# A chunk of a linear-attention kernel loaded as two transfers of whole rows from two queues

## The chip, the cores and the metric

The kernel runs on one core of one Trainium2 chip. The metric is the device time of one execution in microseconds (us); the kernel before takes 338.18 us, the median of three runs (337.67 to 339.53).

## The reference

Two layers follow each other. The first is a linear attention with a decaying state (the form known from RWKV), for 4 batches, 8 heads, 768 positions and a head size of 48; the second is a mixture of 8 experts over the 3072 rows that come out of it, where each row with a positive skip score goes to the one expert that its logits choose.

```python
for t in range(S):                                    # attention, S = 768
    cur = einsum('bhd,bhe->bhde', u[None] * kt, vt)   # kt, vt, rt, wt: (b, h, d) at t
    y[:, :, t] = einsum('bhd,bhde->bhe', rt, state + cur)
    state = wt[:, :, :, None] * state + einsum('bhd,bhe->bhde', kt, vt)
...
e_idx = argmax(xc @ w_gate, axis=1)                   # experts, rows with x @ w_skip > 0
h = maximum(xc[mask] @ w1[e], 0.0)
y[mask] = gate_w[mask, None] * (h @ w2[e])
out[do_compute] = xc + y
```

## The kernel before

**The work and its tiles.** The attention is done in 24 chunks, one for each batch and each block of 128 positions, in the order of `seq` (L61). A chunk's inputs w, r, k and v lie with the head dimension on the partitions: the eight heads are four pairs side by side in the columns, the even head of a pair on partitions 0 to 47, the odd one on 64 to 111 (partitions 48 to 63 and 112 to 127 are zeroed once at the start and never loaded). In DRAM the host keeps, for each chunk and each half g, 48 rows of RW = 2056 floats: w (columns 1 to 516), r, k and v (512 columns each) and three columns of padding. V_OFF = 1541 is where v begins.

**The loads.** `load_chunk(i)` (L126) brings chunk i with four transfers, all on SyncE's queue: for each half the columns ahead of v into one of three tiles `wrk`, then for each half the 512 columns of v into one of four tiles `vt`. Chunk 0 is brought in pieces of 128 rows from a copy of its own, by SyncE's and ScalarE's queues in turn. `load_v` (L143) brings the same v once more with the positions on the partitions, as TensorE needs it. A transfer waits until the last reader of its tile is done. The framework gives the transfers of SyncE's and ScalarE's queues eight semaphores in turn, so that each of them also waits until the one eight places before it has landed.

**The order of the attention stage.** The loop over s (L545) is a pipeline written out by hand inside `tc.manual_schedule()`, so each engine runs its instructions in the order of the code. In step s:

- the loads for chunk s+4 (L548) and v of chunk s+3 are issued; `store(s-1)` (L360) copies the router's columns (lgs) and the output row (x) on ScalarE, and SyncE stores x;
- TensorE and ScalarE carry the state from chunk s to s+1: `update` (L320), then `carry` (psu, sblk; L330, L335);
- VectorE does the scan q of chunk s+2 (L242), kq (L250), the scan rh (L255) and rp (L259); GpSimd does rk (L262) after rp. q, kq, rh, rp and rk read `wrk`; so does ScalarE's check (L274, tile junk);
- TensorE does the outputs of chunk s (L342, L347), which start on the bonus of that chunk, then ScalarE evicts them (xT, L352);
- TensorE does psT, psA and psB of chunk s+1 (L284, L292, L307); VectorE masks psA (two asb, L298) and multiplies psB by `vt` into the bank psY: the bonus of chunk s+1 (L311), the last reader of that chunk's v; TensorE does the output rows of chunk s (psX, L357).

A router (`router`, L370) runs for each group of six chunks; `drip` puts its small VectorE instructions between the others. In 12 of the steps ScalarE splits off the high part of a slice of the first experts' weights (L86), and GpSimd subtracts it (L87).

**The experts.** After the attention the rows are gathered by their expert (indirect transfers of GpSimd's queue) and go through the eight experts (L684), on TensorE for the most part; the change does not touch this stage. `general_path` is for unusual inputs and isn't run here.

**The start.** `setup` (L183) issues chunk 0 and v of chunk 0, zeroes `wrk1` on VectorE (L188) and, on GpSimd, `vt1`, `wrk2`, `vt2`, `vt3` and other tiles (L191 to L204); the load of chunk 1 stands after `vt1`'s memset. The constants c_sb come in two transfers, the second (L552) behind the loads of chunks 1 and 2.

## Time and profile before

| what | before |
|---|---|
| median of three runs | 338.18 us |
| the profiled execution | 338.03 us, of which 336.2 us are its span |
| busy over the span: TensorE, VectorE, ScalarE, GpSimd | 300.8, 253.4, 174.6, 85.9 us |
| mean granted TensorE clock | 0.951 |
| transfers on SyncE's queue for `wrk` and `vt`, chunks 1 to 23 | 46 of 288.9 KB, 46 of 96.0 KB |

The span runs from the first to the last instruction of the profiled execution; the rest of its 338.03 us lies around it. PE is TensorE, PEld its weight loads, DVE VectorE, ACT ScalarE, POOL GpSimd, SP SyncE; an engine's name with a q (SPq, ACTq) marks its sequencer, which waits and issues transfers. A line like "DVE q L242 <- DMA wrk<-wrk" in the waits says that VectorE sat idle ahead of the instruction of line 242 that writes q until a transfer into wrk landed. In a timeline each row is start, duration, engine, line, operation, output<-inputs, shape and count, and in brackets the engine's idle time before it. Matmul ends are modelled, and a releaser is inferred from semaphore events.

### The profile page before, as it was taken

What the parts mean: (1) busy time and instruction counts of PE and PEld (TensorE: products, weight loads), DVE (VectorE), ACT (ScalarE), POOL (GpSimd) and SP (SyncE); (2) the same over time, 40 slices, a digit from 0 to 9 for tenths busy, and PEclk for the clock granted to TensorE, in tenths of its full rate; (3) what the DMA queues carried; (4) which work ended last, traced back from release to release, by engine and by line L of the source; (5) the groups of instructions that cost most, each with busy time, mean ns of one, the idle gap of its engine ahead of it and who ended that gap; (6) DMA issues with size and microseconds to landing.
All of it is one profiled execution on the core that took longest, in us unless ns stands there. A gap on an engine that the chain in (4) does not pass through costs nothing.

```text
span 336.2 us, 7539 instructions
## 1 busy us (share of the span) xinstructions
PE 300.8 (89%) x2845; PEld 279.7 (83%) x2845; DVE 253.4 (75%) x472; ACT 174.6 (52%) x479; POOL 85.9 (26%) x88
## 2 busy tenths in 40 slices
PE   7499998898979989599696999999999999999990
PEld 2388887897869878488585999999999999999990
DVE  5899999899998999999524357859494949585410
ACT  4357666586384864556612255838282828273300
POOL 7312124433233334211200177240202020111111
PEclk9789999799997999979969899999999999999996
DMA  8999999999999887783301149984736373630000
GB/s 234 247 228 216 252 249 263 242 244 210 187 283 254 179 186 162 149 221 111 110 2 47 25 128 329 391 289 144 259 112 261 106 257 126 256 153 23 7 27 12
DMA packets 23104, 60.40 MB, mean 180 GB/s; under 512 B 4103, under 2 KB 10667, under 8 KB 23057
## 3 DMA queue, kind: packets, MB, share of 16 engines
q1 hardware_dynamic: 20576, 53.69, 59.4%
q0 software_dynamic: 2048, 5.48, 4.9%
q10 hardware_dynamic: 432, 0.66, 0.6%
q8 instruction: 24, 0.39, 0.5%
q14 instruction: 24, 0.19, 0.2%
HBM read 52.76 MB, written 7.86 MB: 180 GB/s over the span
## 4 chain that ended last, share of the span: by engine, by line
PE 59%; DMA 19%; DVE 9%; issue 5%; POOL 4%; SPq 2%; ACT 0%; POOLq 0%; DVEq 0%
DMA vt<-wrk 10%; DMA wrk<-wrk 7%; PE psO L735 6%; PE psO L733 6%; PE psO L734 6%; PE psH L715 6%; PE psH L714 6%; PE psH L713 6%; PE psY L342 4%; PE psY L347 3%; PE psA L292 3%; PE psB L307 3%; PE psH L112 3%; POOL rk L262 2%; DVE asb L298 2%
## 5 line engine op out<-in xcount | busy, mean ns | idle before, releaser
L262 POOL TENSOR_TENSOR rk<-wrk 128x512 f32<-128x512 f32 x24 | 30.7, 1279 | 105.8 <-PE psA L292 31.8
L720 ACT ACTIVATE hh<-psH 128x256 fp32r<-128x256 f32 x60 | 23.0, 383 | 55.8 <-PE psH L715 52.5
L715 PE MATMUL psH<-xTh,w1l 128*128 128x256 f32 x168 | 47.5, 283 | 0.0
L714 PE MATMUL psH<-xTl,w1h 128*128 128x256 f32 x168 | 47.5, 283 | 0.0
L713 PE MATMUL psH<-xTh,w1h 128*128 128x256 f32 x168 | 47.5, 283 | 0.0
L677 POOL DMA_INDIRECT out<-fin,ids x16 | 16.8, 1049 | 101.6 <-DVE fin L740 94.7
L342 PE MATMUL psY<-asb,v 128*48 128x128 f32 x384 | 28.2, 294 | 14.2 <-DVE psY L311 14.1
L733 PE MATMUL psO<-w2h,hh 128*128 128x384 f32 x120 | 40.7, 339 | 0.0
L298 DVE TENSOR_TENSOR asb<-psA,c_sb 128x512 f32<-128x512 f32 x48 | 30.8, 683 | 12.8 <-PE psA L292 12.8
L735 PE MATMUL psO<-w2h,hl 128*128 128x384 f32 x120 | 40.1, 334 | 0.0
L734 PE MATMUL psO<-w2l,hh 128*128 128x384 f32 x120 | 40.1, 334 | 0.0
L242 DVE TENSOR_TENSOR_SCAN q<-wrk,smask 128x516 f32<-128x516 f32 x24 | 34.4, 1435 | 3.7 <-DMA wrk<-wrk 3.7
L342 PEld LDWEIGHTS psY<-asb,v 128*48 128x48 f32 x384 | 21.9, 132 | 16.2 <-DVE psY L311 15.7
L721 DVE SCALAR_TENSOR_TENSOR hl<-psH,hh 128x256 fp32r<-128x256 f32 x60 | 25.2, 420 | 12.2 <-ACT hh L720 11.8
L715 PEld LDWEIGHTS psH<-xTh,w1l 128*128 128x128 f32 x168 | 32.2, 192 | 0.0
L714 PEld LDWEIGHTS psH<-xTl,w1h 128*128 128x128 f32 x168 | 32.2, 192 | 0.0
L713 PEld LDWEIGHTS psH<-xTh,w1h 128*128 128x128 f32 x168 | 32.2, 191 | 0.0
L292 PE MATMUL psA<-rp,kq 64*128 64x128 f32 x384 | 29.6, 296 | 1.2 <-DVE rp L259 1.2
L740 DVE SCALAR_TENSOR_TENSOR fin<-psO,gates,xg 128x384 f32<-128x384 f32 x15 | 9.3, 618 | 28.3 <-PE psO L735 28.3
L292 PEld LDWEIGHTS psA<-rp,kq 64*128 64x128 f32 x384 | 25.0, 199 | 5.7 <-issue 3.9
L255 DVE TENSOR_TENSOR_SCAN rh<-wrk,dstart 128x516 f32<-128x516 f32 x24 | 29.3, 1223 | 0.0
L87 DVE TENSOR_TENSOR w2l<-r,w2h 128x512 fp32r<-128x512 f32 x42 | 27.8, 687 | 1.1 <-ACT w2h L86 0.2
(137 smaller groups left out, 658.3 us busy)
## 6 DMA issues: line engine op xcount, KB each, us to landing
r<-w SPq DMA_DIRECT2D x48, 512.0 KB, 5.6
wrk<-wrk SPq DMA_DIRECT2D x46, 288.9 KB, 5.9
v<-vN SPq DMA_DIRECT2D x24, 192.0 KB, 5.6
out<-x SPq DMA_DIRECT2D x24, 192.0 KB, 5.0
vt<-wrk SPq DMA_DIRECT2D x46, 96.0 KB, 5.7
wrk<-wrk SPq DMA_DIRECT2D x1, 258.5 KB, 3.9
wrk<-wrk ACTq DMA_DIRECT2D x1, 256.0 KB, 4.1
wrk<-wrk SPq DMA_DIRECT2D x1, 256.0 KB, 4.6
```

Source lines behind the costliest of these rows:

```text
L242: nc.vector.tensor_tensor_scan(q.rearrange("p a j -> p (a j)")[:, ::-1], t[:, 1:1 + n_][:, ::-1], smask_f[:, ::-1], 0.0, op0=ALU.mult, op1 ...
L255: nc.vector.tensor_tensor_scan(rh.rearrange("p a j -> p (a j)"), wk["w"][:, 0:NP * CW], dstart.rearrange("p a j -> p (a j)"), 0.0, op0=ALU ...
L262: mul = nc.gpsimd.tensor_tensor(rk.rearrange("p a j -> p (a j)"), wk["w"][:, R_OFF:K_OFF], wk["w"][:, K_OFF:V_OFF], op=ALU.mult)
L292: nc.tensor.matmul(wk["psa"][g][:, a], wk["kq"][rows, a], wk["rp"][rows, a], start=True, stop=True)
L298: nc.vector.tensor_tensor(s, wk["psa"][g], tri.rearrange("p (o j) -> p o j", o=1).to_broadcast([P, NP, P]), op=ALU.mult)
L342: nc.tensor.matmul(psy[64 * g:64 * g + D, a], v[:, 2 * a + g], wk["asb"][g][:, a], start=False, stop=(c == 0), skip_group_check=True)
L713: nc.tensor.matmul(ps, w1h[:, o:o + P], xTh[:, kc], start=(kc == 0), stop=False)
L714: nc.tensor.matmul(ps, w1h[:, o:o + P], xTl[:, kc], start=False, stop=False)
L715: nc.tensor.matmul(ps, w1l[:, o:o + P], xTh[:, kc], start=False, stop=(kc == KC - 1))
L733: nc.tensor.matmul(pso, h[j, fc][0], w2h[:, o], start=(fc == 0), stop=False)
L734: nc.tensor.matmul(pso, h[j, fc][0], w2l[:, o], start=False, stop=False)
L735: nc.tensor.matmul(pso, h[j, fc][1], w2h[:, o], start=False, stop=(fc == FC - 1))
```

## The change

There are now four tiles `wrk` of all 2056 columns, and no `vt`. A chunk comes by two transfers, each of 48 whole rows of 8224 bytes: the half on partitions 0 to 47 by SyncE's queue, the half on 64 to 111 by ScalarE's. The bonus reads v from the chunk's `wrk` tile. The tile of chunk s+4 is that of chunk s, so a load now waits for the bonus of chunk s (where the `wrk` half of it waited for rk of chunk s+1 and the check). Chunk 3 has a tile of its own from the start. Line numbers of the code behind `load_chunk` fall by four to six in the changed kernel; the prediction uses those of before.

```diff
--- before.py
+++ after.py
@@ -118,27 +118,23 @@
 
     with tc.tile_pool(name="att", bufs=2) as att, \
             tc.tile_pool(name="pers", bufs=1) as pers:
-        NBUF = 3
-        wrk_sb = [pers.tile([P, V_OFF], F32, name=f"wrk{i}") for i in range(NBUF)]
-        vt_sb = [pers.tile([P, NP, P], F32, name=f"vt{i}") for i in range(NBUF + 1)]
+        NBUF = 4
+        wrk_sb = [pers.tile([P, RW], F32, name=f"wrk{i}") for i in range(NBUF)]
         v_sb = {}
 
         def load_chunk(i):
             b, c = seq[i]
             t = wrk_sb[i % NBUF]
-            vf = vt_sb[i % (NBUF + 1)].rearrange("p a j -> p (a j)")
             if i == 0:
                 nc.sync.dma_start(t[:, :R_OFF], wrk0[:, :R_OFF])
                 nc.scalar.dma_start(t[:, K_OFF:V_OFF], wrk0[:, K_OFF:V_OFF])
                 nc.sync.dma_start(t[:, R_OFF:K_OFF], wrk0[:, R_OFF:K_OFF])
                 nc.scalar.dma_start(c_sb[:, :C_IOTA], cst[:, :C_IOTA])
                 nc.sync.dma_start(u_sb, uP)
-                nc.scalar.dma_start(vf, wrk0[:, V_OFF:V_OFF + NP * P])
+                nc.scalar.dma_start(t[:, V_OFF:], wrk0[:, V_OFF:])
                 return
-            for g in range(2):
-                nc.sync.dma_start(t[64 * g:64 * g + D], wrk[b, c, g, :, :V_OFF])
-            for g in range(2):
-                nc.sync.dma_start(vf[64 * g:64 * g + D], wrk[b, c, g, :, V_OFF:V_OFF + NP * P])
+            nc.sync.dma_start(t[:D], wrk[b, c, 0])
+            nc.scalar.dma_start(t[64:64 + D], wrk[b, c, 1])
 
         def load_v(i):
             b, c = seq[i]
@@ -192,11 +188,9 @@
             nc.gpsimd.memset(smask, Q_MIN)
             nc.gpsimd.memset(smask[:, :, P:CW], 1.0)
             nc.gpsimd.memset(dstart, 0.0)
-            nc.gpsimd.memset(vt_sb[1], 0.0)
             load_chunk(1)
-            nc.gpsimd.memset(wrk_sb[2], 0.0)
-            for i in range(2, NBUF + 1):
-                nc.gpsimd.memset(vt_sb[i], 0.0)
+            for i in range(2, NBUF):
+                nc.gpsimd.memset(wrk_sb[i], 0.0)
             for i in range(2):
                 nc.gpsimd.memset(sblk[i], 0.0)
             nc.gpsimd.memset(onesb, 1.0)
@@ -308,7 +302,9 @@
                                  start=True, stop=True)
 
         def bonus(i):
-            nc.vector.tensor_tensor(psy, work[i]["psb"], vt_sb[i % (NBUF + 1)], op=ALU.mult)
+            nc.vector.tensor_tensor(psy.rearrange("p a j -> p (a j)"),
+                                    work[i]["psb"].rearrange("p a j -> p (a j)"),
+                                    wrk_sb[i % NBUF][:, V_OFF:V_OFF + NP * P], op=ALU.mult)
 
         def update(i):
             b, c = seq[i]
```

SyncE's queue at the start, before, from the first load of chunk 1 on (waits in brackets; DMAHW0 to DMAHW7 are the eight semaphores of transfers):

```order
L139 DMA wrk1_84<-wrk 48x1541 [waits DVE_49]
L139 DMA wrk1_84<-wrk 48x1541 [waits DMAHW0_49]
L141 DMA vt1_87<-wrk 48x512 [waits DMAHW1_49,Pool_49]
L141 DMA vt1_87<-wrk 48x512 [waits DMAHW2_49]
L139 DMA wrk2_85<-wrk 48x1541 [waits DMAHW3_49,Pool_49]
L139 DMA wrk2_85<-wrk 48x1541 [waits DMAHW4_49]
L141 DMA vt2_88<-wrk 48x512 [waits DMAHW5_49,Pool_49]
L141 DMA vt2_88<-wrk 48x512 [waits DMAHW6_49]
L146 DMA v1_169<-vN 128x384 [waits DMAHW7_49]
L552 DMA c_sb_93<-cst 128x360 [waits DMAHW0_49]
```

The same place now:

```order
L136 DMA wrk1_84<-wrk 48x2056 [waits DMAHW0_49,DVE_49]
L136 DMA wrk2_85<-wrk 48x2056 [waits DMAHW1_49,Pool_49]
L142 DMA v1_160<-vN 128x384 [waits DMAHW2_49]
L548 DMA c_sb_90<-cst 128x360 [waits DMAHW4_49]
L549 DMA wgp_sb_97<-wgp 128x420 [waits DMAHW6_49]
L136 DMA wrk3_86<-wrk 48x2056 [waits DMAHW7_49,Pool_49]
```

Eight transfers have become two (ScalarE has the other two), the memset of vt1 is no longer waited for, and the second constants follow chunk 2 and v1. SyncE's half of wrk1 now waits for the landing of the transfer eight places before it.

ScalarE's queue in one step of the attention stage, before (from the check's last copy of one step to the check of the next):

```order
L276 COPY q0all_103<-q2_258 128x4 [waits DVE_49]
L365 COPY lgs0_320<-psX0_309 128x36 [waits PE_49]
L367 COPY x0_322<-psX0_309 128x384
L330 ACTIVATE psu_108<-psu_108,q2_258 128x48 [waits PE_49,Activation_49]
L330 ACTIVATE psu_108<-psu_108,q2_258 128x48 [waits Activation_49] x3
L335 COPY sblk0_110<-psu_108 64x4x48 [waits Activation_49]
L335 COPY sblk0_110<-psu_108 64x4x48
L352 COPY xT1_362<-psY_109 128x512 [waits DVE_49,PE_49]
L286 COPY kt2_369<-psT2_364 128x512 [waits PE_49]
L274 ACTIVATE junk3_391,viol_102<-wrk0_83,bias_lo_90 128x512 [waits DMAHW3_49,DMAHW2_49]
```

The same place now:

```order
L270 COPY q0all_100<-q2_245 128x4 [waits DVE_49]
L137 DMA wrk1_84<-wrk 48x2056 [waits DMAHW5_49,DVE_49,Pool_49]
L361 COPY lgs0_305<-psX0_296 128x36 [waits PE_49]
L363 COPY x0_307<-psX0_296 128x384
L326 ACTIVATE psu_105<-psu_105,q2_245 128x48 [waits PE_49,Activation_49]
L326 ACTIVATE psu_105<-psu_105,q2_245 128x48 [waits Activation_49] x3
L331 COPY sblk0_107<-psu_105 64x4x48 [waits Activation_49]
L331 COPY sblk0_107<-psu_105 64x4x48
L348 COPY xT1_347<-psY_106 128x512 [waits PE_49]
L280 COPY kt2_354<-psT2_349 128x512 [waits PE_49]
L268 ACTIVATE junk3_376,viol_99<-wrk3_86,bias_lo_87 128x512 [waits DMAHW7_49]
```

A transfer into wrk1 (chunk 5, issued in step 1) stands ahead of lgs and x, and waits for VectorE's bonus of chunk 1 and for GpSimd's rk of that chunk. Nothing else has moved on this engine; on VectorE and TensorE the order is the same throughout.

## The prediction

> **What bounds the kernel now.** I read the page first. Its chain of waits names the two transfers that the change touches at its head:
>
> ```profile
> span 336.2 us, 7539 instructions
> DMA vt<-wrk 10%; DMA wrk<-wrk 7%; PE psO L735 6%; PE psO L733 6%; PE psO L734 6%; PE psH L715 6%; PE psH L714 6%; PE psH L713 6%; PE psY L342 4%; PE psY L347 3%; PE psA L292 3%; PE psB L307 3%; PE psH L112 3%; POOL rk L262 2%; DVE asb L298 2%
> ```
>
> 17% of the span would be 57 us. A chain follows one releaser back at each step and does not ask whether another engine was busy all the while, so I took the busy time of the attention stage by windows next (after the length: PE, PEld, DVE, ACT, POOL, granted clock, DMA share, GB/s).
>
> ```profile
> 14.00:20.00 6.00, 3.91 (x28) 3.21 (x30) 5.97 (x8) 1.46 (x3) 1.63 (x2) 0.50 1.09 273
> 20.00:44.00 24.00, 24.00 (x313) 21.63 (x309) 23.06 (x34) 16.33 (x52) 5.10 (x4) 1.00 0.98 227
> 44.00:164.00 120.00, 106.17 (x1291) 95.05 (x1290) 116.12 (x215) 73.47 (x233) 37.62 (x30) 0.96 0.88 208
> ```
>
> From 20 to 44 TensorE is busy for 24.00 of 24 us; from 44 to 164 VectorE is for 116.12 of 120. The waits say what the rest is: first VectorE's between 12 and 164 us, then one line from the waits of the whole span (total, times, longest).
>
> ```profile
> DVE asb L298 <- PE psA L292: 3.3, 7, 1.4
> DVE short L482 <- PE psC L480: 0.3, 1, 0.3
> ...
> DVE q L242 <- DMA wrk<-wrk: 3.7, 2, 2.2
> ```
>
> After 12 us VectorE waits for no load at all. The 3.7 us for wrk are two waits at the very start, for chunk 0 and chunk 1. So the stage is bound by VectorE and TensorE; the loads run beside them, whatever the chain says, and the expert stage behind them is not touched.
>
> **The change part by part.** *The start.* VectorE's timeline, with the idle time in brackets; then TensorE's, SyncE's and ScalarE's rows that bear on it.
>
> ```profile
> 8.61 0.22 DVE L593 CAST trib<-c_sb 128x128 bf16<-128x128 f32 x1
> 10.34 1.23 DVE L242 TENSOR_TENSOR_SCAN q<-wrk,smask 128x516 f32<-128x516 f32 x1 [1.51 <-DMA wrk<-wrk]
> ...
> 15.35 0.69 DVE L311 TENSOR_TENSOR psY<-psB,vt 128x512 f32<-128x512 f32 x1
> 15.94 2.21 DVE L242 TENSOR_TENSOR_SCAN q<-wrk,smask 128x516 f32<-128x516 f32 x1
> ...
> 20.74 1.28 DVE L298 TENSOR_TENSOR asb<-psA,c_sb 128x512 f32<-128x512 f32 x2
> ```
> ```profile
> 16.09 1.95 PE L342 MATMUL psY<-asb,v 128*48 128x128 f32 x16 [4.34 <-DVE psY L311]
> ...
> 19.02 1.62 PE L292 MATMUL psA<-rp,kq 64*128 64x128 f32 x16
> ```
> ```profile
> 2.60 2.53 SPq L139 DMA_DIRECT2D wrk<-wrk  x2
> ```
> ```profile
> 0.75 0.41 ACTq L132 DMA_DIRECT2D wrk<-wrk  x1
> ...
> 3.44 0.20 ACT L190 ACTIVATE junk<-bias_lo 128x1 f32<-128x1 f32 x1
> ```
>
> Chunk 1's scan starts at 10.34 after 1.51 us of waiting, and without another gap VectorE comes to the first bonus (15.35), which TensorE awaits at 16.09. A later landing of chunk 1 moves all of that; an earlier one by at most 1.51. SyncE's two wrk halves are issued between 2.60 and 5.13, the second held until a transfer eight places before it has landed; SyncE's one half will be held likewise, so it goes out no earlier than that second one, at some 4.7. ScalarE's half goes out behind L190, at about 3.6. The memset of wrk1 on VectorE, before both, grows from 1541 to 2056 columns:
>
> ```profile
> 1.17 1.34 DVE L188 MEMSET wrk<- 128x1541 f32 x1 [0.29 <-issue]
> ```
>
> 1.34 × 2056/1541 = 1.79, so it ends at 2.96, ahead of ScalarE's 3.6: covered. What changes is the amount. The scan waits for 2 × 48 rows of 6164 B today, 592 KB, and for 2 × 48 rows of 8224 B then, 790 KB, since v rides along. The rates by window:
>
> ```profile
> 4.00:6.00 2.00, 2.00 (x6) 0.76 (x5) 1.23 (x1) 0.00 (x0) 2.00 (x5) 1.00 1.04 358
> 6.00:7.00 1.00, 1.00 (x4) 0.28 (x3) 0.94 (x3) 0.76 (x2) 0.74 (x5) 1.00 1.27 408
> 7.00:9.00 2.00, 0.78 (x8) 0.55 (x10) 1.79 (x3) 1.42 (x5) 0.22 (x1) 1.00 0.94 194
> ```
>
> Until 7 us the transfers of 128 rows move at 358 to 408 GB/s; from 7 to 9, when only 48-row halves are in the air, at 194. 592/194 is 3.05 us. If two queues bring no more, 790/194 = 4.07: 1.0 us later. If the two halves together move like a transfer of 128 rows, 790/358 = 2.21: 0.85 earlier. Nearest is the mix of half rows and others in the window 20:44, 227 GB/s: 790/227 = 3.48, 0.4 later. I take +0.4 on VectorE. Of this TensorE feels less, as its clock is 0.50 until about 20 us (window 14:20) and a late start loses only half-speed work: +0.3, ends −0.85 and +1.0.
>
> The Trainium skill speaks against the change here. "SBUF — State Buffer", section "Can I just issue two DMAs to hit both halves?", says that two transfers, one at partition 0 and one at 64, ran only 6% faster together than one alone; 194 would become 206 GB/s, 790/206 = 3.83, and the start would cost +0.8 in place of +0.4 on VectorE, the sum be 339.0. Its "Door 1" section has a tile of 64 partitions at 196 GB/s against 328 for 128; the trace agrees (194 against 358 to 408). No run yet shows two such halves at once.
>
> *ScalarE.* It gets 23 issues, each at the head of a step, waiting for the bonus of the chunk whose buffer is refilled. Behind it on ScalarE stand lgs and x (the output row), psu and sblk (the state), xT, kt and the weight slice L86. A step while TensorE is the bound:
>
> ```profile
> 28.59 0.19 ACT L365 COPY lgs<-psX 128x36 f32<-128x36 f32 x1 [1.62 <-PE psX L357]
> 28.67 0.49 ACT L367 COPY x<-psX 128x384 f32<-128x384 f32 x1
> 29.15 1.20 ACT L330 ACTIVATE psu<-psu,q 128x48 f32<-128x48 f32 x4
> 30.39 0.64 ACT L335 COPY sblk<-psu 64x192 f32<-64x192 f32 x2
> 31.05 0.58 ACT L352 COPY xT<-psY 128x512 f32<-128x512 f32 x1
> ```
> ```profile
> 27.87 0.70 DVE L311 TENSOR_TENSOR psY<-psB,vt 128x512 f32<-128x512 f32 x1
> ...
> 33.82 0.70 DVE L311 TENSOR_TENSOR psY<-psB,vt 128x512 f32<-128x512 f32 x1
> ```
> ```profile
> 33.46 1.04 PE L357 MATMUL psX<-wgp_sb,xT 128*128 128x105 f32 x8
> ```
>
> The bonus ends at 28.57, and an issue takes 0.41 (ACTq row above), so lgs starts at about 29.03 and not 28.59. xT ends 0.44 later, at 32.07, and TensorE wants it at 33.46: covered by 1.4 us. Where VectorE is the bound the bonus is late, lgs and x no longer run ahead of it, and xT comes 0.46 (wait and issue) + 0.08 + 0.48 + 1.24 + 0.66 (start to start in the rows above) = 2.9 us after the bonus. There the weight slices matter: GpSimd's L87 needs L86, and a scan that meets L87 is slow (the group on the page, then the line's spread, min/median/max in ns).
>
> ```profile
> L242 DVE TENSOR_TENSOR_SCAN q<-wrk,smask 128x516 f32<-128x516 f32 x24 | 34.4, 1435 | 3.7 <-DMA wrk<-wrk 3.7
> ...
> L242 DVE TENSOR_TENSOR_SCAN q<-wrk,smask x24: 1166/1223/2215, 4.7 to 158.1; 128x516 f32<-128x516 f32 x24
> ```
> ```profile
> 66.33 0.69 DVE L311 TENSOR_TENSOR psY<-psB,vt 128x512 f32<-128x512 f32 x1
> ...
> 73.14 1.59 DVE L242 TENSOR_TENSOR_SCAN q<-wrk,smask 128x516 f32<-128x516 f32 x1
> ```
> ```profile
> 69.71 0.58 ACT L352 COPY xT<-psY 128x512 f32<-128x512 f32 x1
> ...
> 71.67 0.62 ACT L86 CAST w2h<-r 128x512 fp32r<-128x512 f32 x1
> ```
> ```profile
> 71.10 1.28 POOL L262 TENSOR_TENSOR rk<-wrk 128x512 f32<-128x512 f32 x1 [4.21 <-DMA wrk<-wrk]
> 72.37 1.27 POOL L87 TENSOR_TENSOR w2l<-r,w2h 128x512 fp32r<-128x512 f32 x1
> ```
>
> Here xT starts 2.69 after the bonus (67.02); with 2.9 L86 ends at 72.5 instead of 72.29, just behind rk's end, and L87 shifts by 0.15 to 0.2, which the scan at 73.14 pays. Of the 12 slices I found two that tight; the others have about half a microsecond. I take +0.4. The ends: all 12 scans at 2.215 instead of 1.223 would be +11.9, of which some 4 are paid already, so +8 (34.4 − 24 × 1.223 = 5.0 over the median, 1.0 of it chunk 2's); and −4 if every slice came to lie behind its scan.
>
> *The loads of the stage.* Chunk s+4 is now issued after bonus s and scanned two steps later: 2 × 5.95 us (33.82 − 27.87) = 11.9.
>
> ```profile
> DMA to landing us min/median/max: 3.6/5.9/9.3
> ```
>
> The slowest wrk load took 9.3, so 2.6 us of cover are left at the worst: 0. SyncE's v load and output store stand behind the waiting load; v has three steps, and no gather reads a store before chunk 17's: 0. *The rest at nothing:* 69 fewer issues on SyncE, which nobody on VectorE awaits; the bonus reads the same 128x512; GpSimd's memsets at the start grow by a third (2 × 2056 columns for 1541 + 3 × 512), covered as it then waits for the first rp anyway. The constants land earlier, so that chunk 2's scan (15.94) may take 1.22 and not 2.21; but the masks behind it start at 20.74, just as TensorE ends psA (19.02 + 1.62), so that gain ends at 0.1.
>
> Sum: 338.03 (the profiled execution: span 336.2 and 1.83 around it; the median 338.18 is 0.15 above) + 0.3 + 0.4 = 338.7, say 338.6 with the small gain.
>
> **The rivals.** *ScalarE blocks (slower).* If issues there take what SyncE's slow ones did,
>
> ```profile
> L139 SPq DMA_DIRECT2D wrk<-wrk x46: 310/346/1521, 2.6 to 141.9; - x46
> ```
>
> 1.52 in place of 0.41, or if the wait is passed on, L86 slips by over its half microsecond, and L87 lies on the scan in most of the 12 steps: 0.2 to 0.35 each, +2.4 to +4.2 in place of the +0.4: 340.7 to 342.5. It decides from a slip of about 0.5 us. For it: ScalarE's chain is full there; against: the median issue is 0.35. 17%. *The transfers pace the stage (faster).* The DMA share is 0.98 from 20 to 44 us, and the chain names them. All they could give is VectorE's idle time, 0.9 + 3.9, and 1.5 at the start: 338.0 − 6.3 = 331.7 at best, some 335 in part. Against: no wait. 7%. *Only the start gains:* both halves at 358, −0.85, chunk 2's 0.1, and ScalarE covered throughout: 337.1; 8%. *The change doesn't do what it says:* the two queues take turns, so chunk 1 comes 1.0 later: 338.03 + 1.0 + 0.4 = 339.4; 10%. The forecast keeps 58%.
>
> **How the numbers follow.** This kernel's runs tell a change of 0.5% (1.7 us, so 336.5 and 339.9) from none. Faster: the pacing rival's 7% and a third of the start's: 10%. Slower: ScalarE's 17% and 3% from the tails: 20%. Same: 70%. The range leaves out the pacing rival below and the upper half of ScalarE's above, with a little of the tails: 336.4 to 341.0.
>
> **What would show it.** Chunk 1's scan at 10.7 (9.5 to 11.3) instead of 10.34; no DMA in VectorE's waits after 12 us; VectorE again about 116 of 120 us from 44 to 164; scans' mean near 1.43 us; lgs about 0.45 later behind the bonus. A DMA or ACT line in the waits of VectorE, scans well above 1.5 us in the mean, or a stage shorter by over 2 us would prove me wrong.

## The result, and the profile after

The changed kernel takes 342.18 us (median of 14 runs, 340.07 to 344.48), the kernel before 338.08 (median of 14 runs on the same chip, 337.17 to 339.58). The ratio is 1.0108, with a 95% interval of 1.0089 to 1.0127: 1.1% slower, 3.0 to 4.3 us. The forecast was 338.6, with 341.0 as the upper end, so the time lies above the whole range. Ratios here and below leave out single executions that lie more than 1.5% above the fastest of their kernel.

The head of the page after, and its chain by engine:

```profile
span 340.6 us, 7445 instructions
...
PE 60%; DVE 27%; DMA 5%; issue 5%; ACT 1%; POOL 1%; POOLq 0%; DVEq 0%; SPq 0%
```

The chain's share for DMA falls to 5%, from 19% before (10% and 7% of it for the two transfers that the change touches), and the kernel is slower. The percentages say which releaser came last, not what the work costs. The same stretch of VectorE's timeline that the prediction showed, now after:

```profile
13.34 1.23 DVE L236 TENSOR_TENSOR_SCAN q<-wrk,smask 128x516 f32<-128x516 f32 x1 [4.67 <-DMA wrk<-wrk]
...
18.35 0.69 DVE L305 TENSOR_TENSOR psY<-psB,wrk 128x512 f32<-128x512 f32 x1
18.95 1.22 DVE L236 TENSOR_TENSOR_SCAN q<-wrk,smask 128x516 f32<-128x516 f32 x1
...
23.83 1.29 DVE L292 TENSOR_TENSOR asb<-psA,c_sb 128x512 f32<-128x512 f32 x2 [0.99 <-PE psA L286]
```
```profile
19.10 1.95 PE L338 MATMUL psY<-asb,v 128*48 128x128 f32 x16 [7.50 <-DVE psY L305]
```

Chunk 1's scan starts at 13.34 instead of 10.34, the first bonus at 18.35 instead of 15.35, TensorE's psY at 19.10 instead of 16.09: 3.0 us, handed on whole. Chunk 2's scan then takes 1.22 instead of 2.21, but the 0.99 that it gains is lost again: the masks behind it wait 0.99 for TensorE. Why TensorE is late there, the windows show (length, PE, PEld, DVE, ACT, POOL, granted clock, DMA share, GB/s), after first:

```profile
14.00:20.00 6.00, 0.90 (x10) 0.89 (x12) 5.93 (x9) 0.40 (x3) 0.00 (x0) 0.50 1.00 186
20.00:24.00 4.00, 3.80 (x30) 2.91 (x26) 2.94 (x6) 3.02 (x9) 3.09 (x3) 0.58 1.09 208
24.00:44.00 20.00, 19.97 (x250) 18.15 (x252) 18.80 (x28) 12.79 (x42) 5.04 (x4) 1.00 0.95 212
44.00:164.00 120.00, 108.04 (x1301) 96.40 (x1299) 115.16 (x207) 72.77 (x232) 36.75 (x29) 0.93 0.84 213
```

and before, for the windows that are compared:

```profile
20.00:24.00 4.00, 4.00 (x61) 3.59 (x57) 3.93 (x8) 1.80 (x8) 1.28 (x1) 1.00 1.01 212
...
84.00:88.00 4.00, 3.50 (x41) 3.02 (x38) 3.96 (x7) 1.40 (x6) 1.27 (x1) 1.00 0.81 174
100.00:104.00 4.00, 3.31 (x27) 3.12 (x28) 3.97 (x9) 0.99 (x3) 0.00 (x0) 0.74 1.05 257
...
125.00:129.00 4.00, 3.50 (x40) 3.02 (x37) 3.96 (x7) 1.80 (x7) 2.50 (x2) 1.00 0.55 134
```

From 20 to 24 us TensorE ran at full clock before and runs at 0.58 after: with the late start it has 0.90 us of work from 14 to 20, not 3.91, and its half clock ends 3.4 us later. From 44 to 164 VectorE is about as busy in both kernels (115.16, before 116.12). The scans, too, cost what they did:

```profile
L236 DVE TENSOR_TENSOR_SCAN q<-wrk,smask 128x516 f32<-128x516 f32 x24 | 34.6, 1440 | 6.2 <-DMA wrk<-wrk 4.7 <-POOL wrk L193 1.5
```

No load is waited for in the stage. VectorE's two largest waits from 12 to 164 us; the one for DMA is that of chunk 1's scan at 13.34:

```profile
DVE asb L292 <- PE psA L286: 5.4, 9, 1.0
DVE q L236 <- DMA wrk<-wrk: 4.7, 1, 4.7
```

How far the scans of the changed kernel stand behind those of before, from the two timelines:

| scan of chunk | before, us | after, us | behind by |
|---|---|---|---|
| 1 | 10.34 | 13.34 | 3.00 |
| 10 | 66.93 | 70.38 | 3.45 |
| 13 | 86.99 | 91.72 | 4.73 |
| 16 | 107.82 | 110.48 | 2.66 |
| 19 | 127.88 | 132.37 | 4.49 |
| 23 | 158.10 | 162.95 | 4.85 |
| span | 336.2 | 340.6 | 4.4 |

Three microseconds are there from the first step on. After that the distance moves up and down by whole microseconds. Call step k the time from the scan of chunk k to the next: in steps 12 and 18 the distance grows by 1.1 us each. There the masks wait for TensorE, and its clock is halved:

```profile
89.64 1.29 DVE L292 TENSOR_TENSOR asb<-psA,c_sb 128x512 f32<-128x512 f32 x2 [1.03 <-PE psA L286]
```
```profile
84.00:88.00 4.00, 3.25 (x22) 2.90 (x23) 3.97 (x9) 2.20 (x8) 0.00 (x1) 0.60 0.61 132
100.00:104.00 4.00, 3.06 (x44) 2.71 (x40) 3.93 (x9) 3.13 (x10) 1.79 (x2) 1.00 0.99 258
...
125.00:129.00 4.00, 3.57 (x24) 3.05 (x24) 3.97 (x8) 2.20 (x8) 0.00 (x0) 0.59 0.69 156
```

Before, the windows at 84 and 125 had full clock and the one from 100 to 104 had not: there the masks of step 15 waited 1.4 us, which after doesn't have. (Step 14 of before was longer as well, by 1.1 us: a small operation of the router, dsk, met GpSimd's L87 and took 1.31 us instead of 0.20.) In windows of 1 us, the half clock of both traces comes in stretches of 3.4 us or twice or three times that. The Trainium skill, "TensorE: Matmul & The Clock Gate", section "What's actually happening", has a free-running window of 3.41 us in which TensorE's activity decides on half or full clock; the traces agree in the length. Which idle stretch falls into a window shifts with every microsecond of the start, so single differences of 1 us between two profiles of this stage are not evidence of a cause. That holds for the 1.4 us by which the spans differ beyond the start, until runs decide. It holds for the start too. In the profiles of the experiments below, seven kernels with chunks 1 to 3 loaded as before and chunk 1's scan at 10.3 to 10.7 us (before, c1, c2, d1, d2, d3, e1) go to half clock anywhere from 9.8 to 16.2 us and stay there for 3.4 to some 10 us in all. What goes with a late start is the end: they are back at full clock at 19.6 to 21.2 us, and the five with that scan at 12.7 us or later (after, a3, a4, b2, e2) at 23.2 to 24.2; a1 and b3 lie between, at 22.4 and 22.6.

Now the loads of the start. ScalarE's and SyncE's issues of chunk 1, and the time from issue to landing of those transfers (the rows of two narrow windows of the transfers; x2 are SyncE's halves of chunks 1 and 2):

```profile
3.08 0.34 ACTq L137 DMA_DIRECT2D wrk<-wrk  x1
...
6.94 0.32 ACTq L137 DMA_DIRECT2D wrk<-wrk  x1
```
```profile
4.74 0.84 SPq L136 DMA_DIRECT2D wrk<-wrk  x2
```
```profile
wrk<-wrk ACTq DMA_DIRECT2D x1, 385.5 KB, 7.5
```
```profile
wrk<-wrk SPq DMA_DIRECT2D x1, 385.5 KB, 8.6
```

The issues are where the prediction had them or earlier (3.08 for 3.6, 4.74 for 4.7). But ScalarE's half lands at 3.08 + 7.5 = 10.6 and SyncE's at 4.74 + 8.6 = 13.3. From 6 to 9 us both queues moved data, ScalarE's (q10) and SyncE's (q1; packets, MB, share):

```profile
q10 hardware_dynamic: 102, 0.44, 63.1%
q1 hardware_dynamic: 139, 0.31, 47.1%
```

From 9.5 to 12.5 us they did this:

```profile
q1 hardware_dynamic: 113, 0.51, 103.1%
q10 hardware_dynamic: 3, 0.00, 0.1%
```

and from 13 to 18 us this:

```profile
q10 hardware_dynamic: 102, 0.70, 79.5%
q1 hardware_dynamic: 114, 0.17, 21.8%
```

0.51 MB in the 3 us from 9.5 is 170 GB/s, all in SyncE's queue; ScalarE's moves next to nothing, though its half of chunk 2 was sent at 6.94, and has its turn from 13 us on, behind what SyncE had sent until 6.49. From 9.5 us on the two queues did not run side by side: what had been sent first had the first turn. That order alone doesn't explain the delay, since chunk 1's halves were sent ahead of those of chunks 2 and 3. The rate fell as well: from 8 to 14 us all queues together moved 184 GB/s, where before has 218. What holds SyncE's half until 13.3 the trace doesn't show. The constants pay as well, 12.9 us to landing where before had 5.1:

```profile
c_sb<-cst SPq DMA_DIRECT2D x1, 180.0 KB, 12.9
```

### The profile page after: what moved, and what is told of

The parts are those of the page before. It is cut to its first block, busy times and chain, and to the rows that moved or that the text cites. A ratio compares the mean times of both kernels' runs of the same rounds, so it can differ in the third digit from the quotient of the medians.

```text
span 340.6 us, 7445 instructions
## 1 busy us (share of the span) xinstructions
PE 303.1 (89%) x2845; PEld 281.7 (83%) x2845; DVE 253.4 (74%) x472; ACT 173.6 (51%) x479; POOL 88.2 (26%) x86
## 3 DMA queue, kind: packets, MB, share of 16 engines
q10 hardware_dynamic: 1904, 9.74, 12.9%
## 4 chain that ended last, share of the span: by engine, by line
PE 60%; DVE 27%; DMA 5%; issue 5%; ACT 1%; POOL 1%; POOLq 0%; DVEq 0%; SPq 0%
PE psO L731 6%; PE psO L730 6%; PE psO L729 6%; PE psH L711 6%; PE psH L710 6%; PE psH L709 6%; DVE q L236 6%; DVE rh L249 5%; PE psY L343 4%; DVE asb L292 4%; PE psY L338 4%; DMA wrk<-wrk 4%; PE psH L112 4%; PE psA L286 3%; DVE rp L253 3%
## 5 line engine op out<-in xcount | busy, mean ns | idle before, releaser
L338 PE MATMUL psY<-asb,v 128*48 128x128 f32 x384 | 29.5, 303 | 15.6 <-DVE psY L305 15.5
L236 DVE TENSOR_TENSOR_SCAN q<-wrk,smask 128x516 f32<-128x516 f32 x24 | 34.6, 1440 | 6.2 <-DMA wrk<-wrk 4.7
L338 PEld LDWEIGHTS psY<-asb,v 128*48 128x48 f32 x384 | 22.9, 136 | 17.6 <-DVE psY L305 17.1
L286 PE MATMUL psA<-rp,kq 64*128 64x128 f32 x384 | 28.9, 292 | 1.2 <-DVE rp L253 1.2
L286 PEld LDWEIGHTS psA<-rp,kq 64*128 64x128 f32 x384 | 24.3, 195 | 5.8 <-issue 4.1
L87 DVE TENSOR_TENSOR w2l<-r,w2h 128x512 fp32r<-128x512 f32 x42 | 27.9, 689 | 1.0
```

The costliest lines, as they stand in the source:

```text
L236: nc.vector.tensor_tensor_scan(q.rearrange("p a j -> p (a j)")[:, ::-1], t[:, 1:1 + n_][:, ::-1], smask_f[:, ::-1], 0.0, op0=ALU.mult, op1 ...
L286: nc.tensor.matmul(wk["psa"][g][:, a], wk["kq"][rows, a], wk["rp"][rows, a], start=True, stop=True)
L338: nc.tensor.matmul(psy[64 * g:64 * g + D, a], v[:, 2 * a + g], wk["asb"][g][:, a], start=False, stop=(c == 0), skip_group_check=True)
```

## The experiments

The theory from these traces: the late landing of chunk 1 is what the change costs, about 3 of the 3.7 us (ratio 1.0108 of 338.1); the rivals are ScalarE's waits in the stage, and chance in the half clock. Each kernel was timed against the kernel before on the same chip. In the first comparison and in the groups a, d and e before takes 338.1 to 338.7 us; on the chip that ran b and c it takes 350.0 (there the time from the last scan to the end of the span is 188 to 190 us in the profiles, where before had 178). Ratios are therefore compared, not times.

**a1: chunk 1 as before.** In `load_chunk`, ahead of the two new transfers:

```diff
+            if i == 1:
+                for g in range(2):
+                    nc.sync.dma_start(t[64 * g:64 * g + D, :V_OFF], wrk[b, c, g, :, :V_OFF])
+                for g in range(2):
+                    nc.sync.dma_start(t[64 * g:64 * g + D, V_OFF:], wrk[b, c, g, :, V_OFF:])
+                return
```

> The changed kernel, with chunk 1 alone loaded as the kernel before loads it: w, r and k of both halves first, v behind them, all on SyncE's queue. Start theory (chunk 1's late landing costs about 3 of the 4.1 us, because v travels along in the rows that the first scan waits for): chunk 1's scan goes from 13.34 back to 10.3 to 11.0 us, and the time to 339.0 to 339.6. Rival, ScalarE's early transfers (the halves of chunks 2 and 3 that ScalarE may now send at once take the rate from chunk 1): the scan stays at 12 or later and the time at 341 or more. Rival, ScalarE's waits in the stage cost most of the 4.1 us: the scan returns, but the time stays above 340.5.

```profile
10.51 1.23 DVE L242 TENSOR_TENSOR_SCAN q<-wrk,smask 128x516 f32<-128x516 f32 x1 [1.73 <-DMA wrk<-wrk]
```

340.79 us, ratio 1.0065 (1.0036 to 1.0094). The scan is back, although ScalarE sends its half of chunk 2 at 6.80. The time is not: it is above the theory's 339.0 to 339.6, and above the 340.5 that the rival with ScalarE's waits named. Something besides chunk 1's landing costs 1 to 3 us in this kernel. Part of it may still be the start: chunk 3's scan comes at 23.65, 1.1 behind before (22.53). In c1 below, which loads chunks 2 and 3 too as before, it comes at 22.68, and the ratio is 1.0031.

**a2: all on SyncE's queue.** `nc.scalar.dma_start(t[64:64 + D], ...)` becomes `nc.sync.dma_start(...)`.

> The changed kernel with both halves of every chunk on SyncE's queue, so whole rows and four buffers, but nothing on ScalarE's. If ScalarE's early transfers are what delays chunk 1: its scan at 11.0 to 11.5 (790 KB at 194 GB/s, 1.0 behind 10.34). If it is the amount and the rows alone: 13.3 again. If ScalarE's issues cost 1 us in the steps at the groups' ends and behind: that us goes as well. Both together: 338.5 to 339.5; only the start's: 339.5 to 340.5; only ScalarE's: 341.0 to 341.4; neither: 342.2.

```profile
11.43 1.23 DVE L236 TENSOR_TENSOR_SCAN q<-wrk,smask 128x516 f32<-128x516 f32 x1 [2.50 <-DMA wrk<-wrk]
```

340.71 us, just above what was named for the start alone; ratio 1.0054 (1.0032 to 1.0076). The scan is 1.09 behind before: that is the greater amount at the rate of one queue, the prediction's upper end of 1.0. The four kernels that load chunk 1 by the change's two queues have it at 12.71 (a3), 13.03 (a4), 13.16 (e2) and 13.34 (after), so the other 1.3 to 1.9 us of delay come with the second queue. Again some 0.7 us more than the start remain, with no load on ScalarE's queue after chunk 0's.

**a4: ScalarE's early halves on SyncE's queue.** Only the second halves of chunks 2 and 3:

```diff
-            nc.scalar.dma_start(t[64:64 + D], wrk[b, c, 1])
+            eng = nc.sync if i in (2, 3) else nc.scalar
+            eng.dma_start(t[64:64 + D], wrk[b, c, 1])
```

> The changed kernel with the second halves of chunks 2 and 3 on SyncE's queue, behind chunk 1's; chunk 1 still on both queues, and all from chunk 4 on too. If ScalarE's early halves of chunks 2 and 3 take the rate from chunk 1: chunk 1's scan at 10.5 to 11.5, the time 339.3 to 340.3. If it is the amount that chunk 1 waits for, or its rows of 8224 B: the scan stays at 13.0 to 13.5 and the time at 342.

```profile
13.03 1.23 DVE L237 TENSOR_TENSOR_SCAN q<-wrk,smask 128x516 f32<-128x516 f32 x1 [4.26 <-DMA wrk<-wrk]
```

342.49 us, ratio 1.0092 (1.0060 to 1.0124). It isn't the halves of chunks 2 and 3 that ScalarE sends early. That chunk 1's own two halves come by two queues is enough.

**b1: halves crossed.** Odd chunks as in the change, even chunks with the engines changed over:

```diff
+            qs = (nc.sync, nc.scalar) if i % 2 else (nc.scalar, nc.sync)
-            nc.sync.dma_start(t[:D], wrk[b, c, 0])
-            nc.scalar.dma_start(t[64:64 + D], wrk[b, c, 1])
+            qs[0].dma_start(t[:D], wrk[b, c, 0])
+            qs[1].dma_start(t[64:64 + D], wrk[b, c, 1])
```

> The changed kernel with the halves crossed: of odd chunks SyncE loads rows 0-47 and ScalarE rows 64-111, of even chunks the other way round, so that the two transfers that follow each other in one queue fill opposite halves. Theory: the second half of chunk 1 is slow (13.34 and 13.03, against 11.43 with all on SyncE's queue) because behind it in SyncE's queue comes the same half of chunk 2, and 48 partitions take only some 170 GB/s. Then chunk 1's scan comes at 11.3 to 12.2 and the time falls by 1 to 2 us, to 340.3 to 341.3. Rival: the two queues themselves cost the rate, whichever half they fill: the scan stays at 13.0 to 13.4 and the time at 342.

```profile
12.27 1.23 DVE L237 TENSOR_TENSOR_SCAN q<-wrk,smask 128x516 f32<-128x516 f32 x1 [3.60 <-DMA wrk<-wrk]
```

Ratio 1.0057 (1.0036 to 1.0079). The scan is 0.4 to 1.1 earlier than in the four kernels that load chunk 1 by the change's queues and don't cross (12.71 to 13.34), just behind what the theory gave, and the ratio falls by as much as expected. That fits the theory that the same half twice in a queue is a part of the delay, but it isn't shown: this is one profile on another chip, profiles with the start of before have their scan anywhere from 10.34 to 11.55, and the transfers alone (b4) don't bear the theory out.

**b4: transfers alone.** The whole computation is left out; groups of transfers into two buffers. After each group VectorE reads column 0 of both buffers, and the next transfer into a buffer waits for that read.

> No computation of the reference at all: only transfers of the inputs into two buffers, each group landed before the next is sent, two repetitions, and zeros written out. One half (385.5 KB) alone; both halves by one queue and by two; the same half of two buffers by one queue and by two; four halves in the orders of the change and of its neighbours; 128 rows by one queue and by two. If halves of opposite partitions add up by two queues, a pair by two queues lands in the time of one half. If transfers take turns, a pair takes 385.5 KB at some 200 GB/s longer (1.9 us), by one queue as by two. If the same half twice is slow, its pair takes longer than the pair of opposite halves.

SyncE's issues that begin a group, then VectorE's reads that end them:

```profile
5.61 0.39 SPq L78 DMA_DIRECT2D buf<-wrk  x1
10.21 0.32 SPq L81 DMA_DIRECT2D buf<-wrk  x1
...
16.83 0.31 SPq L85 DMA_DIRECT2D buf<-wrk  x1
...
79.96 0.33 SPq L128 DMA_DIRECT2D buf<-wrk  x1
```
```profile
10.03 0.21 DVE L64 COPY got<-buf 128x1 f32<-128x1 f32 x2 [4.29 <-DMA buf<-wrk]
16.65 0.22 DVE L64 COPY got<-buf 128x1 f32<-128x1 f32 x2 [6.40 <-DMA buf<-wrk]
23.22 0.21 DVE L64 COPY got<-buf 128x1 f32<-128x1 f32 x2 [6.36 <-DMA buf<-wrk]
...
85.54 0.21 DVE L64 COPY got<-buf 128x1 f32<-128x1 f32 x2 [5.55 <-DMA buf<-wrk]
```

One half alone takes 10.03 − 5.61 = 4.42 us from issue to landing; both halves by one queue (L81) 6.44, by two queues (L85) 6.39; in the second repetition 4.45, 7.00 and 6.33. A second queue brings nothing: the pair takes 1.9 to 2.6 us longer than a half either way. It costs nothing either, so the 1.3 to 1.9 us that come with it in the kernel have a cause that these pairs don't show.

The last group (L128) is both halves by one queue in two blocks of columns, w, r and k ahead of v. VectorE's read follows 5.58 us after the first issue in both repetitions, but it reads only column 0, which comes with w: that is when w, r and k have landed. The last block of v, issued at 81.26, lands 4.9 us later, 6.2 us after the group's first issue (6.1 in the second repetition). So whole rows are hardly slower than the two blocks, 0.2 to 0.9 us; what the blocks give is w, r and k, which the scan waits for, 0.8 to 1.4 us sooner. A group that the rows above don't show is 128 rows, 1028.0 KB, in two blocks of columns by two queues (L124, L125): 5.1 and 4.9 us from first issue to last landing, for a third more bytes than the pair.

The groups with two buffers overlapped with their neighbours and aren't clean. As they stand they don't agree on b1's theory: the same half of two buffers by one queue takes 7.33 and 7.23 us, somewhat more than the opposite halves, but a buffer of which each queue brings a half lands after 6.09 and 6.18 us in the order of the change and after 7.41 and 7.45 crossed.

**b2: a late start alone.** The kernel before, with w, r and k of chunk 2 (and chunk 1's v) sent ahead of w, r and k of chunk 1:

```diff
-            for g in range(2):
-                nc.sync.dma_start(t[64 * g:64 * g + D], wrk[b, c, g, :, :V_OFF])
+            if i < 3:
+                wrk_halves(3 - i)
+            else:
+                wrk_halves(i)
```

> The kernel before, with nothing changed but that w, r and k of chunk 2 are sent ahead of those of chunk 1 (and the memsets of the two buffers changed over): a late first load by itself. Chunk 1's scan should come at about 13.3 to 13.9 instead of 10.3. Start theory: the whole delay is passed on, with another 3.4 us of half clock, and the time is 341.2 to 342.5, as with the change. Rival: VectorE makes most of it up later, so that the time stays under 340, and what the change costs is in its stage.

```profile
14.33 1.24 DVE L250 TENSOR_TENSOR_SCAN q<-wrk,smask 128x516 f32<-128x516 f32 x1 [5.54 <-DMA wrk<-wrk]
```

Ratio 1.0079 (1.0049 to 1.0110), 2.8 us (1.7 to 3.8), nearer to the start theory than to its rival. Kernels with the start of before had this scan at 10.40 (c1), 10.64 (c2) and 11.55 (b3, in the longest of its twelve executions) on this chip, so it was 2.8 to 3.9 late. A late start is paid for, most of it by these numbers, with nothing else changed.

**b3: ScalarE sends, nothing else.** The kernel before; from chunk 4 on ScalarE sends the second half of w, r and k:

```diff
+            nc.sync.dma_start(t[:D], wrk[b, c, 0, :, :V_OFF])
+            (nc.scalar if i > 3 else nc.sync).dma_start(t[64:64 + D], wrk[b, c, 1, :, :V_OFF])
```

> The kernel before, with the second half of w, r and k sent by ScalarE from chunk 4 on; three buffers, split columns and the start are those of before. If ScalarE's issues and their waits cost what the prediction gave them: 338.5 to 339.1 where before has 338.1 to 338.7, that is 0.4 more. If they cost 1 us or more: 339.5 or more. If nothing: within 0.3 of before. ScalarE's issue waits for the buffer's last reader there, which is not the bonus, so only the issues and the queueing are the same as in the change.

Ratio 0.9991 (0.9964 to 1.0019). Twenty issues on ScalarE cost nothing that can be measured. Their wait for the bonus isn't in it.

**a3: ScalarE's half behind the state's copies.** From chunk 4 on the transfer is sent behind `carry(s)`, not at the head of the step:

```diff
                     carry(s)
+                    if s + 4 < n:
+                        second_half(s + 4)
```

> The changed kernel; from chunk 4 on ScalarE's half is issued behind the state's copies (psu, sblk) of the step instead of at its head, so that lgs, x, psu and sblk no longer wait for the bonus. The start is left as it is (scan of chunk 1 at 13.3). If the wait at ScalarE's head costs about 1 us (steps 12, 18, 21 and 22): 341.0 to 341.4. If that difference is chance in where the weight slices meet the scans: 341.9 to 342.5. Slower than 342.5 if the later issue makes a load late, with DMA in VectorE's waits after 20 us.

```profile
55.68 1.80 DVE L242 TENSOR_TENSOR_SCAN q<-wrk,smask 128x516 f32<-128x516 f32 x1 [0.20 <-DMA wrk<-wrk]
...
78.69 1.23 DVE L242 TENSOR_TENSOR_SCAN q<-wrk,smask 128x516 f32<-128x516 f32 x1 [2.02 <-DMA wrk<-wrk]
```

345.34 us, ratio 1.0148 (1.0106 to 1.0190): the outcome named as slower than 342.5. These are the scans of chunks 8 and 11. ScalarE's halves of them go out at 45.78 and 67.98, 2.5 and 5.2 us behind the end of the bonus that frees the buffer (43.25 and 62.73). So a delay about as long as the 2.6 us of cover that the prediction had counted uses it up, and twice as much makes VectorE wait 2 us.

**c1, c2: the stage alone, and the buffers alone.** c1 is a1 with `if i < 4` for `if i == 1`: the start of before up to chunk 3, then the change. c2 has the change's four buffers, and every chunk loaded as before.

> The changed kernel with chunks 1 to 3 loaded in the parts, the order and the queue of before; from chunk 4 on whole rows by the two queues, four buffers, as changed: the stage of the change with the start of before. Start theory: within 0.4% of before at most (0 to +1 us), chunk 1's scan as early as in before. Rival, the stage costs too (chunk 1 alone as before left +0.65%): 0.5 to 0.8% slower than before although chunk 1 comes on time.

> The changed kernel's four buffers of whole rows (v beside w, r and k, the bonus reading it there), every chunk loaded in the parts, the order and the queue of before. If what was left over with chunk 1 as before and with all on SyncE's queue is due to the transfers of whole rows or to ScalarE: within 0.3% of before. If it is due to the buffers themselves: 0.5% slower.

c1: ratio 1.0031 (1.0006 to 1.0056), with its scan of chunk 1 at 10.40. c2: 0.9997 (0.9965 to 1.0029). The changed stage costs 1.1 us (0.2 to 2.0), the layout of the buffers nothing that can be measured. With b2's 2.8 for the start, the two parts make 3.9; the change cost 3.65 (3.0 to 4.3).

**d1, d2, d3, e1: what the stage costs.** All have the start of before. d1 is c1 with both halves on SyncE's queue; d2 is c2 with ScalarE's issues as in b3; d3 is c1 with `NBUF = 5`, so that the load of chunk s+4 finds a buffer whose last reader is a step earlier; e1 is d1 with `NBUF = 5`.

> As the run of the stage alone (start of before, from chunk 4 on whole rows in four buffers), but both halves on SyncE's queue. That run was 0.31% slower than before (0.06 to 0.56). If ScalarE's wait for the bonus is what costs there (in its profile the scans of chunks 10, 11, 16 and 17 were 0.11 to 0.17 longer than in before): 0 to 0.15%, with these scans at 1.22, 1.59, 1.22 and 1.58 again wherever the half clock falls as in before. If whole rows cost by themselves: 0.3% again.

> The four buffers loaded in the parts and the order of before (within 0.3% of before as it was), but the second half of w, r and k is sent by ScalarE from chunk 4 on; that part's buffer is free when the product r*k on GpSimd is done, so ScalarE does not wait for the bonus. If it is the wait that costs: 0 to 0.15%. If the issue on ScalarE costs by itself: 0.3% or more.

> The stage alone (start of before, whole rows by the two queues from chunk 4 on) with five buffers instead of four, so that the buffer of chunk s+4 was read a step earlier and ScalarE's issue finds it free. If the wait at the head of ScalarE's step costs: 0 to 0.15% where four buffers gave 0.31%, and lgs and psu as early in the step as in before. If the transfers by two queues cost: 0.3% again.

> The stage on SyncE's queue alone (start of before, whole rows from chunk 4 on; 0.44% slower than before with four buffers), with five buffers, so that no load waits for the bonus of the same step. If late, waiting loads are the rest: within 0.2% of before. If whole rows by one queue are: 0.3 to 0.5% again.

| whole rows from chunk 4 on | four buffers | five buffers |
|---|---|---|
| two queues | c1 1.0031 (1.0006 to 1.0056) | d3 1.0000 (0.9978 to 1.0022) |
| SyncE's queue | d1 1.0044 (1.0021 to 1.0066) | e1 0.9995 (0.9967 to 1.0023) |

d2: 0.9989 (0.9958 to 1.0021). ScalarE's wait is not the cause, since d1 has nothing of these loads on ScalarE and costs no less. It does lengthen single scans, as expected: those of chunks 10 and 11 take 1.33 and 1.76 us in c1 and again 1.22 and 1.59 in d1, as in before, but the time did not come back with them. Whole rows as such aren't either, since they cost nothing with a fifth buffer. What the four have in common points to the wait: a load of whole rows that has to wait for the bonus of the same step costs something, on whichever queue. Each pair ran on two chips and its intervals touch or overlap, so this is the likeliest reading, no more. By what path 1 to 1.5 us would come of it stays open: in the profiles of c1 and d1 VectorE waits for no load after chunk 1's.

**e2: the whole change with five buffers.** `NBUF = 5` in the changed kernel.

> The whole change with five buffers instead of four; the start as with the change (chunk 1's scan at 12.7 to 13.4). If the start costs 2.8 to 3.3 us and the waiting loads the rest: 0.8 to 1.0% slower than before, where four buffers gave 1.08%. If the fifth buffer changes nothing: 1.1% again.

Ratio 1.0118 (1.0080 to 1.0156), from five runs. No gain over the change's 1.0108 is seen, where the last table would give 0.3% to 0.5%; the interval hardly excludes it. So a gain from the fifth buffer is seen with the start of before only, and the reading of the table stays unproven for the change itself.

**c3: chunk 1 earlier.** The kernel before, chunk 1 from an array of 128 rows like chunk 0, w first; the memsets of its two tiles are left out.

> The kernel before with one change of another kind: chunk 1 comes, like chunk 0, from an array with 128 rows (zeros in the unused ones), w first, then k, r and v, all on SyncE's queue. If the start is what counts and 128 rows move at 358 to 444 GB/s: chunk 1's scan waits for 258 KB and starts 1.2 to 1.5 us earlier than in before, without a wait, and the time falls by 0.8 to 1.5 us (0.2 to 0.45%). If a start that is earlier is lost again in half clock: within 0.2%.

```profile
8.78 1.23 DVE L246 TENSOR_TENSOR_SCAN q<-wrk,smask 128x516 f32<-128x516 f32 x1
```

Ratio 0.9995 (0.9965 to 1.0025). The scan starts 1.6 earlier, without a wait, and nothing comes of it: chunk 5's scan starts at 34.75, where before had 34.43. The trace shows where it goes. Chunk 1's kq takes 1.48 us (before 0.66) and chunk 2's rh 2.29 (before 1.22), each while GpSimd's rk runs beside it, where before only chunk 2's q was slow (2.21, here 1.22); then VectorE waits 0.2 us for TensorE's psA and 0.4 ahead of the bonus. TensorE's clock is 0.50 from 14 to 20 here too, and until 21.4 us (before, until 20.0). So the early start is lost in part on VectorE itself and in part, it seems, in the half clock; the two were not told apart. A late start isn't lost: it is there in the time (b2), and the half clock ends later then.

**c4, e3: one transfer of 128 rows for each chunk.** The changed kernel, every chunk from an array of 128 rows (1053 KB with zeros, 1028.0 KB as the profile counts) in one transfer on SyncE's queue; c4 with four buffers, e3 with five. The memsets of the buffers, which nothing needs now, are left out.

```diff
-            nc.sync.dma_start(t[:D], wrk[b, c, 0])
-            nc.scalar.dma_start(t[64:64 + D], wrk[b, c, 1])
+            nc.sync.dma_start(t, wrk0[i])
```

> The changed kernel with every chunk in one transfer of 128 rows (1053 KB with the zeros) on SyncE's queue, four buffers, nothing on ScalarE. If the rows of the chunks' halves are what makes the start late: chunk 1's scan at 10 to 11 us, 2 to 3 us earlier than with the change, and the time within 0.3% of before. If the greater amount (a third more) wins: scan at 12 or later, loads late in the stage, and slower than before by 0.5% or more.

> One transfer of 128 rows for each chunk on SyncE's queue (0.44% faster than before with four buffers, 0.11 to 0.77) with five buffers: a candidate for the fastest version. If the waits for the bonus cost there too: 0.5 to 0.8% faster than before. If not: 0.3 to 0.5% again.

```profile
9.86 1.37 DVE L232 TENSOR_TENSOR_SCAN q<-wrk,smask 128x516 f32<-128x516 f32 x1 [0.93 <-DMA wrk<-wrk]
```

c4: ratio 0.9956 (0.9923 to 0.9989); e3: 0.9923 (0.9891 to 0.9956), 336.37 us where before has 338.16. A third more bytes, and chunk 1 is there 3.5 us earlier than with the change. Two things add up in that: from 8 to 14 us all queues together moved 405 GB/s (e3: 415), where the change has 184 and a2 214; and the one transfer goes out at 2.59, where the change's second half is held until 4.74 and that of a2 until 4.93. Both beat both kernels; e3's ratio is what was named for waits that cost, but it was measured on another chip than c4's and their intervals overlap. What of the 2.6 us of e3 is the start, and what the stage, was not told apart. In the profiles the lead is gone at chunk 3's scan (22.62 and 23.12 us, before 22.53), so the early start by itself is not seen to give it.

## Why the prediction was wrong

*What bounds the kernel:* right. VectorE and TensorE bind the stage, no load is waited for there, and the chain's 17% for transfers were not time that this change could win (e3, the fastest version, wins 0.8%).

*The start:* the step that failed. The issues were placed rightly, and "the scan waits for 790 KB" too. The rate was wrong, and with it the term +0.3 of the sum. The prediction took 227 GB/s, with 194 as the slow end, "if two queues bring no more", so +0.4 and +1.0 at most. The scan came 3.0 later: 1.1 of it with all on one queue (a2), as the slow end had it, and 1.3 to 1.9 more with the second queue. In time, a scan that is 2.8 to 3.9 late costs 2.8 us (b2; 1.7 to 3.8). 194 was no lower bound. Whole rows by two queues moved at 170 GB/s from 9.5 to 12.5 us, and SyncE's half landed 2.7 us behind ScalarE's. Why the second queue makes the pair slower in the kernel, and not by itself (b4), stays open. The rival "queues take turns" came nearest to the mechanism, but sized it with the same 194, at 339.4. The sentence on the Trainium skill, "SBUF — State Buffer", section "Can I just issue two DMAs to hit both halves?", pointed the right way; b4 agrees that they serialize (a pair takes 1.9 to 2.6 us longer than a half, by two queues as by one). The 339.0 by its rule was still 3 us short.

*"TensorE feels less, as its clock is 0.50":* in line with an earlier start (c3: 1.6 us, no gain, though not all of that is the clock's doing), wrong for a later one, for which the half clock runs on (0.58 from 20 to 24 us).

*ScalarE:* right in kind. The rows after, for the step at 32 us:

```profile
31.29 0.69 DVE L305 TENSOR_TENSOR psY<-psB,wrk 128x512 f32<-128x512 f32 x1
```
```profile
32.05 0.36 ACTq L137 DMA_DIRECT2D wrk<-wrk  x1
32.46 0.19 ACT L361 COPY lgs<-psX 128x36 f32<-128x36 f32 x1 [1.75 <-PE psX L353]
```

lgs starts 0.48 behind the bonus's end (31.98), as forecast (0.45), and the scans' sum is 34.6 against 34.4. The +0.4 put on it is not borne out: b3 and d2 give nothing, without the wait for the bonus, and what the stage costs, d1 has without ScalarE. An effect as small as 0.4 us lies within their intervals. The rival "ScalarE blocks", at 340.7 to 342.5, would have fitted the time for a cause that wasn't there.

*The loads of the stage at 0:* right about VectorE's waits, and a3 shows that the 2.6 us of cover were about what there was (2.5 us of it used up, a wait of 0.2). But c1 and d1 cost 0.3 to 0.4%, which their versions with a fifth buffer don't; that the waiting load could have a price was not in the sum.

*"The constants land earlier":* wrong. They were sent earlier (7.94) and landed at 20.8, since the same queues carried whole rows ahead of them. The gain of chunk 2's scan did end at nothing, as said.

*The size of what one profile can tell:* steps 12, 14, 15 and 18 differ by 1 us each between before and after, by where the half clock falls and by one meeting with L87. The first reading of the result put 1 us on ScalarE from just these steps; b3, d1 and d2 took it back.

## What to carry to other kernels

For halves of 48 rows a second engine's queue added no rate while the first was still moving, and one transfer of 128 rows moved faster than both; what counts at a start is which bytes the first instruction waits for, and what was sent ahead of them. Take the slow end of a rate from the state that the change makes, not from the slowest one in the trace before, or leave the range open on that side. And let runs, not the steps of two single profiles, decide on a microsecond where the clock comes and goes.

## What the runs showed of the hardware

A pair of 48-row halves by itself lands no sooner by two queues than by one (6.39 and 6.33 us against 6.44 and 7.00), and hardly sooner when its rows of 8224 B come in blocks of 6164 B and 2060 B (6.2 and 6.1). 128 rows in two blocks of columns by two queues, a third more bytes, land in 5.1 and 4.9 us. In the running kernel all queues together moved 405 and 415 GB/s from 8 to 14 us with 128 rows for a chunk (c4, e3), a quarter of them zeros, 214 with halves by one queue (a2) and 184 with halves by two (after). TensorE's half clock comes in stretches of 3.4 us or two or three times that, and which stretch falls where differs between profiles of one start (it sets in at 9.8 to 16.2 us). One chip takes 350 us for what the others do in 338, most of it behind the attention stage.
